# Attention followed by hashed experts on one core: rows of x of four sequences kept on the chip and written later, gathers and weight loads in another order

## The chip, the cores and the metric

The kernel runs on one core of a Trainium2 chip. The metric is the time of one execution on the device in microseconds (us), less is better. Shorthand used throughout: PE is TensorE, PEld its weight loads, DVE VectorE, ACT ScalarE, POOL GpSimd, SP SyncE. Sequences are numbered 0 to 7 and experts 0 to 7.

## What is computed

Two stages, the second fed by the first. Attention over 8 sequences of 576 positions and 8 heads of 64, causal by blocks of 64; then each of the 4608 rows of 512 numbers goes through the one expert that its token id selects:

```python
scores = (q @ k.T) / sqrt(64);  scores = where(block_i >= block_j, scores, -1e9)
x   = softmax(scores) @ v                       # 8 sequences x 576 rows, heads side by side: [4608, 512]
e   = token_ids * 2654435761 % 8                # one expert for each row
out = relu(x @ w1[e]) @ w2[e]                   # w1[e]: 512 x 1024, w2[e]: 1024 x 512
```

## The kernel before, in words

**Attention.** One loop (L597) runs over g = 0 to 33. Pair g (two heads of sequence g // 4) is scored at step g in three chunks (`S_chunk`, L225: matmuls on PE, then one exponential on ACT, L237), and multiplied by V two steps later (`PV`, L263), after which `norm` (L281) divides on DVE and puts the rows into a buffer `xs` on the chip. A sequence fills four steps, so the rows of sequence b are complete at step 4b+5. `T_sixth` transposes q and k of the next sequence on PE.

**Loads and stores around it.** K and Q come by POOL's DMA queue (`load_seq`, L547, at the first step of a sequence), V by SP's queue (`load_v`, L135, six transfers into one of two buffers `vf`, then cast by POOL, `cast_v`, L151). Also on SP's queue, `write_x(b)` (L294, called at L641 in step 4b+5) writes the rows of sequence b to `x_dram` in two transfers. There are two buffers `xs`. An engine's queue is followed in program order: an instruction that waits holds up what stands behind it.

**Experts.** Routing gives each expert five tiles of 128 rows: tiles 0 to 2 hold rows of sequences 0 to 5 only, tiles 3 and 4 the remainder. I write (e,t) for tile t of expert e. `load_x` (L304) gathers a tile from `x_dram` by an indirect DMA of POOL: for tiles 0 to 2 it needs the written rows of sequences 0 to 5, for tiles 3 and 4 all rows. `turn_x` (L501) transposes a gathered tile on PE, DVE copies it into `xT`. `stage_a` (L669) is the first product with the ReLU on ACT, `stage_b` (L693) the second, each of its tiles being scattered to the output by an indirect DMA of POOL (L709). `load_w1` and `load_w2` (L483, L488) bring an expert's weights, 2 MB each in HBM, converted to 1 MB of bf16 on the way, by POOL's queue. I write w1(e) and w2(e) for them.

**The join of the two**, in which most of the change lies. In the loop's last steps, on POOL: w1(0) at step 25, held by L647 until a part of V of sequence 7 has landed; cast of V of sequence 7 at step 26; gathers (0,0), (0,1), (0,2), (1,0), (1,1), (1,2) one each at steps 27 to 32, each held until the last exponential of its step (`last`, L617); w1(1) at step 28; w2(0) at step 32; w2(1) at step 33. On PE: `turn_x` of (0,0) and (0,1) at the end of step 30 and of (0,2) at the end of step 31; three of the eight parts of `stage_a` of expert 0 at step 32. Behind the loop (L741 on): the other five parts of `stage_a(0)` with the turns of (1,0), (1,1), (1,2) between them and, on POOL, the gathers (2,0), (2,1), (2,2); then on POOL (0,3), (0,4), (1,3), (1,4); on PE `stage_a(1)` for three tiles, `stage_b(0)` for three tiles with the turns of (0,3), (0,4); then the loop over the experts (L746), which starts with the last two tiles of expert 0. `xT` and `hT` of experts 0 and 1 lie in a pool of their own (`fst`, two buffers), those of later experts in `mx`, which is opened where the attention's buffers were.

Of the kernel before, what the change touches and what calls it, by code (L numbers as in the profile page):

```python
# [11 lines left out]
BF16 = mybir.dt.bfloat16  # L12
# [5 lines left out]
B, H, S, D = 8, 8, 576, 64  # L18
E, DM, FF = 8, 512, 1024
N = B * S  # L20
NT = 4
NP = H // 2
# [3 lines left out]
G = CAP // 128  # L26
# [12 lines left out]
def kernel(  # L39
# [11 lines left out]
    P = nc.NUM_PARTITIONS  # L51
# [6 lines left out]
    xin = ctx.enter_context(tc.tile_pool(name="xin", bufs=3))  # L58
    fst = ctx.enter_context(tc.tile_pool(name="fst", bufs=2))

# [42 lines left out]
    def after(ins, first, why):  # L103
        tc.add_manual_dep(ins.ins, first.ins.name, SYNC, reason=why)
# [14 lines left out]
    pt4s = [fix.tile([P, NP * 64 + 64], BF16, name=f"pt4{z}") for z in range(2)]  # L119
    xss = [fix.tile([P, 5, DM], BF16, name=f"xs{z}") for z in range(2)]  # L120

# [159 lines left out]
    def norm(g):  # L281
        b, r = divmod(g, NP)
        Ov = Os.pop(g)[:, :, 0 : 5 * (D + 1)].rearrange("p m (t c) -> p m t c", t=5)
        rs = rsall[:, g, :, :]
        nc.vector.reciprocal(rs, Ov[:, :, :, D])  # L285
        nc.vector.tensor_tensor(  # L286
            out=xss[b % 2][:].rearrange("p t (m r d) -> p m t r d", m=2, r=NP)[:, :, :, r, :],
            in0=Ov[:, :, :, 0:D], in1=rs[:, :, :, None].to_broadcast([P, 2, 5, D]), op=ALU.mult)

    x_writes, x_reads, xgs = [], [], {}  # L290
    GE = ES // P


    def write_x(b):  # L294
        xs = xss[b % 2]
        for dst, src in (
            (x_dram[b * S : b * S + 512, :].rearrange("(i p) c -> p i c", p=P), xs[:, 0:NT, :]),
            (x_dram[b * S + 512 : (b + 1) * S, :], xs[0:64, NT, :]),
        ):
            ins = nc.sync.dma_start(dst, src)  # L300
            for r in x_reads:
                tc.declare_no_dep(ins.ins, r.ins, reason="early slots hold rows of earlier sequences")

    def load_x(e, g0, g1, first=None):  # L304
# [188 lines left out]
    NPAIRS = B * NP  # L493
# [3 lines left out]
    def new_ffn(e, pool):  # L497
        xTs[e] = pool.tile([P, NKT, CAP], BF16, name="xT", tag="xT")
        hTs[e] = pool.tile([P, NFT, CAP], BF16, name="hT", tag="hT")
# [15 lines left out]

    for e in range(2):
        new_ffn(e, fst)

# [78 lines left out]
    for g in range(NPAIRS + 2):  # L597
# [30 lines left out]
        if g == NPAIRS - 2:  # L628
            for tt in range(GE - 1):
                turn_x(0, tt, psT)  # L630
        if g == NPAIRS - 1:
            turn_x(0, GE - 1, psT)
        if g == NPAIRS:
# [4 lines left out]
        if r == 0 and b + 2 < B:  # L638
            load_seq(b + 2)
        if r == 1 and g > 1:  # L640
            write_x((g - 5) // NP)  # L641

        c = b + 2 if b + 2 < B - 1 else b + 1 if b + 1 == B - 1 else B
        if r == 1 and c < B:
            vparts[c] = load_v(c)
        if r == 1 and c == B - 1:
            after(load_w1(0), vparts[c][1], "these bytes are wanted first")  # L647
        if r == 2 and b + 1 < B:
            cast_v(b + 1)

        gx = g - (NPAIRS - 5)
        if 0 <= gx < 2 * GE:
            load_x(gx // GE, gx % GE, gx % GE + 1, last)
        if g == NPAIRS - 4:
            load_w1(1)
        if g == NPAIRS:
            load_w2(0)
        if g == NPAIRS + 1:
            load_w2(1)
    assert next(rgen, None) is None and rgen.gi_frame is None  # L660
# [58 lines left out]
    def sums_in_range():  # L719
# [19 lines left out]
        nc.vector.tensor_single_scalar(ctl[:, 3:4], nov[:], float(E * G), op=ALU.add)  # L739

    stage_a(0, 0, ES, EARLY, [(1, tt) for tt in range(GE)], [(2, tt) for tt in range(GE)])  # L741
    for e in range(2):
        load_x(e, GE, G)
    stage_a(1, 0, ES)
# [209 lines left out]
```

## Time and profile before

| what | value |
|---|---|
| median of 3 runs | 304.59 us (302.82 to 308.38) |
| the profiled execution, its own time | 303.5 us |
| the same, span from first to last instruction | 301.7 us |
| granted clock of TensorE, mean over the span | 0.972 |
| PE busy | 263.5 us, 87% of the span |
| ACT busy, DVE busy, POOL busy | 148.7, 141.0, 134.7 us |
| DMA | 55.63 MB, 184 GB/s over the span |

The profiled execution has 1.8 us outside its span (303.5 against 301.7). PE is busy for 87% of the span, with a matmul's end modelled, so what counts is where it is idle and what ended that idle time. A line of a timeline gives the start, the duration, the engine, the line of the kernel, the operation with its output and input, how many instructions are merged into it, and in brackets the idle time before it with what ended it.

### The profile page before, as it was taken

The numbers are of one execution on the slowest core, as the hardware profiler recorded it, in microseconds if no ns is written. First come the engines' busy times: TensorE is split into PE (matmuls) and PEld (weight loads), VectorE is DVE, ScalarE is ACT, GpSimd is POOL, SyncE is SP. The second block draws the span as 40 slices with busy tenths as digits, with TensorE's granted clock in tenths as the row PEclk, the third lists the DMA queues.
The fourth block names the chain that finished last, engine by engine and source line by source line (L and its number), as shares of the span: only waits on it lengthen the run. The fifth ranks groups of instructions, "written<-read, shape, count | busy, mean of one in ns | idle before, by whom it ended". The sixth has DMA issues, their size and how long they took to land. (4 is left out here: it accounts for less than half of the span.)

```text
span 301.7 us, 7635 instructions
## 1 busy us (share of the span) xinstructions
PE 263.5 (87%) x3224; PEld 172.8 (57%) x3241; DVE 141.0 (47%) x296; ACT 148.7 (49%) x192; POOL 134.7 (45%) x164
## 2 busy tenths in 40 slices
PE   7778889899989797459959999999999999999992
PEld 2456667676767575246516656657466575665740
DVE  6787788887889693214012242150421504215131
ACT  3698697888987789234604303306034060240610
POOL 8153250514141304652266735674756738435132
PEclk9999999999999999778979999999999999999997
DMA  6999999999999959979924999699796998942012
GB/s 101 205 184 181 224 174 240 192 233 193 223 214 235 176 149 182 230 146 175 233 70 139 189 226 224 226 185 275 157 202 230 192 269 185 219 187 116 36 72 87
DMA packets 65383, 55.63 MB, mean 184 GB/s; under 512 B 39989, under 2 KB 54325, under 8 KB 65344
## 3 DMA queue, kind: packets, MB, share of 16 engines
q0 software_dynamic: 22832, 40.90, 64.9%
q1 hardware_dynamic: 42512, 14.20, 20.8%
q8 instruction: 26, 0.43, 0.6%
q14 instruction: 13, 0.11, 0.1%
HBM read 67.15 MB, written 15.20 MB: 273 GB/s over the span
## 5 line engine op out<-in xcount | busy, mean ns | idle before, releaser
L237 ACT ACTIVATE pt<-ps 128x1024 bf16<-128x1024 f32 x96 | 92.2, 1026 | 23.2 <-PE ps L220 22.4
L683 ACT ACTIVATE hT<-hp 128x640 bf16<-128x640 f32 (+2 forms) x77 | 46.3, 601 | 102.2 <-PE hp L679 101.4
L700 PE MATMUL yp<-w2b,hT 128*128 128x512 bf16 x305 | 75.7, 385 | 0.8
L679 PE MATMUL hp<-xT,w1b 128*128 128x320 bf16 (+2 forms) x500 | 71.8, 298 | 3.0 <-DVE xT L506 2.8
L506 DVE COPY xT<-tx 128x512 bf16<-128x512 bf16 x40 | 17.0, 424 | 107.0 <-PE tx L504 107.0
L709 POOL DMA_INDIRECT out_dram<-ysb,perm x40 | 39.8, 996 | 50.4 <-DVE ysb L707 22.9
L679 PEld LDWEIGHTS <-w1b 128*128 128x128 bf16 x500 | 48.3, 97 | 23.5 <-issue 6.0
L309 POOL DMA_INDIRECT xg<-x_dram,tabi x40 | 41.1, 1027 | 33.0 <-issue 10.7
L700 PEld LDWEIGHTS <-hT 128*128 128x128 bf16 x320 | 30.4, 99 | 30.7 <-issue 1.5
L211 PE MATMUL ps<-qkT 64*128 64x512 bf16 (+4 forms) x320 | 39.0, 300 | 8.1 <-ACT pt L237 5.1
L186 DVE COPY qkT<-tp 128x768 bf16<-128x768 bf16 x42 | 38.3, 951 | 7.8 <-PE tp L179 7.8
L275 PE MATMUL O<-vx,pt 128*128 128x65 bf16 x896 | 40.2, 197 | 1.9 <-DVE xs L286 1.7
L275 PEld LDWEIGHTS <-pt 128*128 128x128 bf16 x896 | 32.6, 99 | 7.9 <-DVE xs L286 2.6
L211 PEld LDWEIGHTS <-qkT 64*128 64x128 bf16 x320 | 19.2, 94 | 22.2 <-issue 9.5
L111 POOL DMA_DIRECT2D kb<-in_k_dram x9 | 6.7, 748 | 53.8 <-PE O L278 25.0
L707 DVE COPY ysb<-yp 128x512 f32<-128x512 f32 x40 | 27.3, 682 | 6.1 <-PE yp L700 6.1
L286 DVE TENSOR_TENSOR xs<-O,rsall 128x640 bf16<-128x640 f32 x32 | 26.4, 824 | 1.1
L504 PE MATMUL tx<-identbf,xg 128*128 128x128 bf16 x160 | 15.9, 225 | 11.3 <-DMA xg<-x_dram,tabi 11.3
L504 PEld LDWEIGHTS <-xg 128*128 128x128 bf16 x160 | 12.5, 101 | 20.6 <-DMA xg<-x_dram,tabi 12.1
L220 PE MATMUL ps<-maskq,maskk 64*128 64x64 bf16 x256 | 23.1, 191 | 0.0
L154 POOL CAST vx<-vf 128x2048 bf16<-128x2048 f32 x8 | 15.3, 1916 | 7.3 <-DMA vf<-in_v_dram 2.8
L285 DVE RECIPROCAL rsall<-O 128x10 f32<-128x10 f32 x32 | 7.0, 219 | 18.8 <-PE O L278 18.0
(142 smaller groups left out, 179.9 us busy)
## 6 DMA issues: line engine op xcount, KB each, us to landing
vf<-in_v_dram SPq DMA_DIRECT2D x32, 256.0 KB, 9.3
w1b<-in_moe_w_dram POOLq DMA_DIRECT2D x8, 1024.0 KB, 8.4
w2b<-in_moe_w_dram POOLq DMA_DIRECT2D x8, 1024.0 KB, 13.6
x_dram<-xs SPq DMA_DIRECT2D x8, 512.0 KB, 9.9
kb<-in_k_dram POOLq DMA_DIRECT2D x7, 576.0 KB, 7.2
qb<-in_q_dram POOLq DMA_DIRECT2D x6, 576.0 KB, 10.1
vf<-in_v_dram SPq DMA_DIRECT2D x16, 64.0 KB, 4.4
qb<-in_q_dram POOLq DMA_DIRECT2D x2, 320.0 KB, 8.1
```

Of the source, the lines that this page charges most:

```text
L186: ins = copy(qk[:, :, w, :].rearrange("p h (g j) -> p h g j", j=JR)[:, :, :, j0 + c0 : j0 + c1], tp[:, at[c0] : at[c1 - 1] + 1, :].rearran ...
L211: nc.tensor.matmul(ps[:, m, o0 : o0 + n], lhsT=qk[rows, r, 1, 128 * i : 128 * i + 128], rhs=qk[rows, r, 0, q0 : q0 + n], start=True, stop= ...
L237: return nc.scalar.activation(ptv[:, :, 512 * ch : 512 * ch + 512], ps[:], ACT.Exp, scale=SCALE)
L275: nc.tensor.matmul(dst, lhsT=pt[:, o0 : o0 + 128], rhs=vx[:, h, i, :], start=(i == 0), stop=(i == t))
L286: nc.vector.tensor_tensor(out=xss[b % 2][:].rearrange("p t (m r d) -> p m t r d", m=2, r=NP)[:, :, :, r, :], in0=Ov[:, :, :, 0:D], in1=rs[ ...
L309: r = nc.gpsimd.indirect_dma_start(out=xgs[e][:, gg, :], out_offset=None, in_=x_dram[0:rows, :], in_offset=bass.IndirectOffsetOnAxis(ap=ta ...
L504: nc.tensor.transpose(out=tp[:, db, :], in_=xgs[e][:, tt, db * P : (db + 1) * P], identity=identbf[:])
L679: nc.tensor.matmul(hp[:, t, 0:n], lhsT=w1b[:, db, ft * P : (ft + 1) * P], rhs=xT[:, db, p0:p1], start=(db == 0), stop=(db == NKT - 1),)
L683: relu = nc.scalar.activation(hT[:, ft, c0:c1].rearrange("p (t n) -> p t n", n=n), hp[:, 0 : len(parts), 0:n], ACT.Relu)
L700: nc.tensor.matmul(yp[:], lhsT=hT[:, ft, tt * P : (tt + 1) * P], rhs=w2b[:, ft, :], start=(ft == 0), stop=(ft == NFT - 1),)
L707: nc.vector.tensor_copy(ysb[:], yp[:])
L709: ins = nc.gpsimd.indirect_dma_start(out=out[:, :], out_offset=bass.IndirectOffsetOnAxis(ap=perm3[:, gg : gg + 1], axis=0), in_=ysb[:], in ...
```

## The change

Eight edits. (1) Five buffers `xs` in place of two; the rows of sequences 2 to 5 stay in them and are all written at step 25, in place of steps 13, 17, 21 and 25. Those of sequences 0, 1, 6 and 7 are written at the steps they had. (2) V of sequence 7 is asked for at step 21 in place of step 25. (3) `fst` has one buffer; `xT` and `hT` of expert 1 come from `mx`. (4) Gathers one step later: (0,0) at step 28 to (1,0) at step 31, with (1,1) and (1,2) both at step 32. (5) w1(0) moves from step 25 to step 28, behind gather (0,0), and loses its hold on V; w1(1) moves from step 28 to step 30, behind gather (0,2). (6) On PE, (0,0) alone is turned at step 30; (0,1) and (0,2) at step 31. (7) w2(1) moves from step 33 to behind the gathers (0,3), (0,4), and waits until the rows of sequence 7 are written; (1,3), (1,4) come behind it. (8) w2(0) keeps step 32, now behind two gathers there.

```diff
--- before.py
+++ after.py
@@ -56,7 +56,7 @@
     dram = ctx.enter_context(tc.tile_pool(name="dram", bufs=1, space=DRAM))
     wts = ctx.enter_context(tc.tile_pool(name="wts", bufs=3))
     xin = ctx.enter_context(tc.tile_pool(name="xin", bufs=3))
-    fst = ctx.enter_context(tc.tile_pool(name="fst", bufs=2))
+    fst = ctx.enter_context(tc.tile_pool(name="fst", bufs=1))
 
     x_dram = dram.tile([N, DM], BF16, name="x_dram")
     a_dram = dram.tile([B * H, S, D], BF16, name="a_dram")
@@ -117,7 +117,8 @@
         vexts.append((vx, v4))
     pts = [fix.tile([P, 2 * PTW + 64], BF16, name=f"pt{z}") for z in range(3)]
     pt4s = [fix.tile([P, NP * 64 + 64], BF16, name=f"pt4{z}") for z in range(2)]
-    xss = [fix.tile([P, 5, DM], BF16, name=f"xs{z}") for z in range(2)]
+    XB = 5
+    xss = [fix.tile([P, 5, DM], BF16, name=f"xs{z}") for z in range(XB)]
 
     def set_fixed():
         for vx, v4 in vexts:
@@ -284,7 +285,7 @@
         rs = rsall[:, g, :, :]
         nc.vector.reciprocal(rs, Ov[:, :, :, D])
         nc.vector.tensor_tensor(
-            out=xss[b % 2][:].rearrange("p t (m r d) -> p m t r d", m=2, r=NP)[:, :, :, r, :],
+            out=xss[b % XB][:].rearrange("p t (m r d) -> p m t r d", m=2, r=NP)[:, :, :, r, :],
             in0=Ov[:, :, :, 0:D], in1=rs[:, :, :, None].to_broadcast([P, 2, 5, D]), op=ALU.mult)
 
     x_writes, x_reads, xgs = [], [], {}
@@ -292,7 +293,7 @@
 
 
     def write_x(b):
-        xs = xss[b % 2]
+        xs = xss[b % XB]
         for dst, src in (
             (x_dram[b * S : b * S + 512, :].rearrange("(i p) c -> p i c", p=P), xs[:, 0:NT, :]),
             (x_dram[b * S + 512 : (b + 1) * S, :], xs[0:64, NT, :]),
@@ -300,6 +301,7 @@
             ins = nc.sync.dma_start(dst, src)
             for r in x_reads:
                 tc.declare_no_dep(ins.ins, r.ins, reason="early slots hold rows of earlier sequences")
+        return ins
 
     def load_x(e, g0, g1, first=None):
         if e not in xgs:
@@ -513,8 +515,7 @@
                 start=(db == 0), stop=(db == NKT - 1))
         nc.scalar.activation(hTs[e][:, ft, 0:ES], hp[:, 0:ES], ACT.Relu)
 
-    for e in range(2):
-        new_ffn(e, fst)
+    new_ffn(0, fst)
 
     J2 = 8
     EARLY = 3
@@ -626,10 +627,10 @@
         turn(0)
 
         if g == NPAIRS - 2:
-            for tt in range(GE - 1):
+            turn_x(0, 0, psT)
+        if g == NPAIRS - 1:
+            for tt in range(1, GE):
                 turn_x(0, tt, psT)
-        if g == NPAIRS - 1:
-            turn_x(0, GE - 1, psT)
         if g == NPAIRS:
             for ft in range(EARLY):
                 stage_a_early(0, ft)
@@ -637,26 +638,22 @@
             next(rgen, None)
         if r == 0 and b + 2 < B:
             load_seq(b + 2)
-        if r == 1 and g > 1:
-            write_x((g - 5) // NP)
-
-        c = b + 2 if b + 2 < B - 1 else b + 1 if b + 1 == B - 1 else B
-        if r == 1 and c < B:
-            vparts[c] = load_v(c)
-        if r == 1 and c == B - 1:
-            after(load_w1(0), vparts[c][1], "these bytes are wanted first")
+        if r == 1 and b + 2 < B:
+            vparts[b + 2] = load_v(b + 2)
+
+        if r == 1:
+            for c in {5: (0,), 9: (1,), 25: (2, 3, 4, 5), 29: (6,), 33: (7,)}.get(g, ()):
+                rows = write_x(c)
         if r == 2 and b + 1 < B:
             cast_v(b + 1)
 
-        gx = g - (NPAIRS - 5)
-        if 0 <= gx < 2 * GE:
-            load_x(gx // GE, gx % GE, gx % GE + 1, last)
-        if g == NPAIRS - 4:
-            load_w1(1)
+
+        for e, tt in {28: ((0, 0),), 29: ((0, 1),), 30: ((0, 2),), 31: ((1, 0),), 32: ((1, 1), (1, 2))}.get(g, ()):
+            load_x(e, tt, tt + 1, last)
+        if g in (28, 30):
+            load_w1((g - 28) // 2)
         if g == NPAIRS:
             load_w2(0)
-        if g == NPAIRS + 1:
-            load_w2(1)
     assert next(rgen, None) is None and rgen.gi_frame is None
     att_ctx.close()
 
@@ -738,9 +735,11 @@
         nc.vector.tensor_scalar(ctl[:, 2:3], nb[:, 0:1], float(-E * G), float(E * G), op0=ALU.mult, op1=ALU.add)
         nc.vector.tensor_single_scalar(ctl[:, 3:4], nov[:], float(E * G), op=ALU.add)
 
+    new_ffn(1, mx)
     stage_a(0, 0, ES, EARLY, [(1, tt) for tt in range(GE)], [(2, tt) for tt in range(GE)])
-    for e in range(2):
-        load_x(e, GE, G)
+    load_x(0, GE, G)
+    after(load_w2(1), rows, "the rows are wanted first")
+    load_x(1, GE, G)
     stage_a(1, 0, ES)
     stage_b(0, 0, GE, [(0, tt) for tt in range(GE, G)])
     for e in range(E):
```

## Rows read from the trace of the kernel before

**Rows 1.** Busy time by stretch: window, five engines (instructions), granted clock, DMA share, GB/s.

```profile
105.00:110.00 5.00, 4.51 (x104) 3.41 (x102) 4.83 (x8) 3.96 (x5) 0.00 (x0) 1.00 0.36 116
...
125.00:130.00 5.00, 3.69 (x43) 2.49 (x44) 0.85 (x2) 1.94 (x2) 1.39 (x2) 0.50 0.99 162
...
155.00:160.00 5.00, 5.00 (x22) 2.21 (x21) 2.14 (x4) 0.00 (x0) 2.75 (x3) 0.66 0.43 131
```

**Rows 2.** Timeline of PE, join of the two stages and the third expert.

```profile
126.31 1.04 PE L504 MATMUL tx<-identbf,xg 128*128 128x128 bf16 x8 [4.48 <-DMA xg<-x_dram,tabi]
...
134.05 0.40 PE L504 MATMUL tx<-identbf,xg 128*128 128x128 bf16 x4 [3.10 <-DMA xg<-x_dram,tabi]
...
135.58 3.39 PE L511 MATMUL hp<-xT,w1b 128*128 128x384 bf16 x12
...
142.37 7.02 PE L679 MATMUL hp<-xT,w1b 128*128 128x384 bf16 x40
...
154.85 0.40 PE L504 MATMUL tx<-identbf,xg 128*128 128x128 bf16 x4 [3.73 <-DMA xg<-x_dram,tabi]
155.08 3.46 PE L700 MATMUL yp<-w2b,hT 128*128 128x512 bf16 x8
...
160.44 4.24 PE L679 MATMUL hp<-xT,w1b 128*128 128x256 bf16 x32
...
193.89 0.39 PE L504 MATMUL tx<-identbf,xg 128*128 128x128 bf16 x4
```

**Rows 3.** Timeline of POOL: DMA issues of weights, gathers, scatters.

```profile
115.02 0.78 POOL L486 DMA_DIRECT2D w1b<-in_moe_w_dram  x1 [13.95 <-DMA vf<-in_v_dram]
...
123.20 0.83 POOL L486 DMA_DIRECT2D w1b<-in_moe_w_dram  x1
...
152.07 1.01 POOL L309 DMA_INDIRECT xg<-x_dram,tabi  x1 [6.91 <-DMA x_dram<-xs]
...
162.57 0.86 POOL L486 DMA_DIRECT2D w1b<-in_moe_w_dram  x1
...
190.54 0.99 POOL L709 DMA_INDIRECT out_dram<-ysb,perm  x1 [4.04 <-DMA w2b<-in_moe_w_dram]
```

**Rows 4.** DMA issues of single transfers, KB each, us from issue to landing.

```profile
w1b<-in_moe_w_dram POOLq DMA_DIRECT2D x1, 1024.0 KB, 8.5
...
w1b<-in_moe_w_dram POOLq DMA_DIRECT2D x1, 1024.0 KB, 10.4
...
w2b<-in_moe_w_dram POOLq DMA_DIRECT2D x1, 1024.0 KB, 9.0
xg<-x_dram,tabi POOLq DMA_INDIRECT x1, 2.8
...
kb<-in_k_dram POOLq DMA_DIRECT2D x1, 576.0 KB, 8.0
```

**Rows 5.** Timeline of SP's queue.

```profile
95.39 13.10 SPq L300 DMA_DIRECT2D x_dram<-xs  x4
...
120.12 21.88 SPq L300 DMA_DIRECT2D x_dram<-xs  x4
```

**Rows 6.** Timeline of ACT: last exponentials of steps 28, 29 and 30.

```profile
116.03 0.41 ACT L250 ACTIVATE pt<-ps 128x256 bf16<-128x256 f32 x1
116.73 5.65 ACT L237 ACTIVATE pt<-ps 128x1024 bf16<-128x1024 f32 x6 [0.29 <-PE ps L220]
```

**Rows 7.** DMA queues over 111-116, 125-131.5 and 143-151 us: packets, MB, share of engines.

```profile
q1 hardware_dynamic: 4067, 1.04, 91.6%
...
q0 software_dynamic: 551, 1.16, 99.9%
...
q0 software_dynamic: 982, 1.23, 78.1%
q1 hardware_dynamic: 608, 0.59, 25.3%
```

**Rows 8.** Timeline of PE: first use of K of sequence 7.

```profile
103.63 0.86 PE L179 MATMUL tp<-identbf,kb 128*64 128x128 bf16 x24 [1.04 <-DMA kb<-in_k_dram]
```

## The prediction, as it was made

> **What bounds the kernel now.** I read the stretches first [rows 1], then PE's timeline where the clock or the DMA share falls, then the queues that feed it. Three things are to be seen.
>
> PE is the bound nearly everywhere, but at the join of the two stages it waits three times for a gather: 4.48 us before 126.31, 3.10 before 134.05, 3.73 before 154.85, 11.3 us in all [rows 2]. After these waits it runs at the lower of its two clocks for a while: granted 0.50 in 125 to 130 and 0.66 over 155 to 160 [rows 1]. The price: twelve matmuls of 384 columns took 3.39 us where forty at full clock took 7.02, so 2.1 for twelve: 1.3 lost; eight of 512 columns took 3.46, by the same rate (512/384 of 0.176 us each) 1.9: 1.6 lost [rows 2]. With about 1.3 after the first wait, the three cost about 4 us more. So of PE's 38.6 us from 121.83 (126.31 less its wait) to 160.44 some 15.5 are no work.
>
> Why the gathers are late is in POOL's queue [rows 3]. w1(0) waited 13.95 us for V of sequence 7, and the cast and gather (0,0) stand behind it. V was itself late: on SP it stands behind the write of sequence 5, which waits for the last row of that sequence (the four transfers of two writes take 13.10 us, to 108.5 [rows 5]), while the DMA engines are 0.36 busy [rows 1]. The second wait is one of order: w1(1), issued at 123.20, landed 10.4 later, at 133.6, and gather (0,2), issued right behind it, was there at 134.05 [rows 2 to 4]: a gather lands behind the weights queued ahead of it. The third: the writes of sequence 7 were issued by 142.0 [rows 5] and POOL saw them landed at 152.07 [rows 3]; w2(0) and w2(1) shared the engines with them.
>
> **The parts, in the order of time** (times on the axis of before).
>
> Writes kept back. A written row packet costs 0.253 x 8 us x 16 / 608 = 0.053 us of one engine [rows 7], so the 576 packets of a sequence 1.9 us of all 16, four sequences 7.7. In steps 13 to 21 they leave the loads alone; I price that at nothing, since K came only 1.0 us late for sequence 7 [rows 8] and the exponentials pace those steps. Bounds: a gain of that 1.0 us, a loss in the rival on K below.
>
> V of sequence 7. It now waits on SP for no row, only for its buffer and V of sequence 6 ahead of it. 4067 packets of V took 91.6% of 5 us [rows 7], so all 4608 take 5.2. SP was through with V of sequence 6 by 95.4 [rows 5]; without writes ahead, I take V of 7 as landed by 100 to 104. POOL's 13.95 us wait goes. Next on SP: sequences 2, 3, 4 go at once, sequence 5 when its last row is there (108.5, as before); at 1.9 us each all four have landed by about 113. Gather (0,0) is asked for only after that.
>
> Gather (0,0). POOL is free; it waits for the last exponential of step 28, done at 116.0 [rows 6]. Alone a gather takes 2.8 [rows 4]: there at 119, and PE turns it at 121.83 without a wait. The 4.48 us go.
>
> w1(0). Issued behind it at 117.1, in place of 115.02. It took 8.5 [rows 4]: 125.6, and the write of sequence 6, issued from 120.12 [rows 5], adds up to 1 us: 126.6. Gathers (0,1), (0,2), issued at 119.6 and 122.4 after the exponentials of steps 29 and 30 (thirds of the 5.65 us [rows 6]), stand behind it: there at 127 to 129, I take 128.0. PE, with one turn at 121.83 and step 31 behind it (2.8 us, half of the 5.65 for two steps' exponentials [rows 6]), is at that turn by 124.6. New wait: 3.4. It is of the length that lowered the clock before, so I add 1.6.
>
> Then on PE: of its 23.1 us of work up to 160.44 (38.6 less 15.5), sixteen parts of stage_a and three tiles of stage_b take 16.8 by the rate above and step 31 2.8, which leaves 3.5 for eight turns and the last two steps' PVs. I take 2.2 of these here, with three parts of stage_a 4.3, and the slow 1.6: 133.9; one part more: 134.5. w1(1) starts on the engines when w1(0) and the two gathers are through, about 126.6; 551 packets took 99.9% of 6.5 us, so its 512 take 6.0 [rows 7], with some 2 to land, and 0.5 for the gather: (1,0) at about 135.4. New wait 0.9. The cover of w1(1) itself is that it is wanted only by stage_a(1).
>
> w2(0). It starts behind (1,2) and, by the 9.0 of before [rows 4] less some 1.5 us from issue to first packet, lands 7.5 after 135, plus 1.9 for the rows of sequence 7: 144.4 to 145. PE has five parts of stage_a(0), three turns and the eight parts of stage_a(1) before it: 144.0. New wait about 0.6. The rows of sequence 7 are issued at 135, not 141, and share with one w2, not two: landed by 143.8 (8.8 us, before 10). (0,3) then lands at 146.7, when PE has its first tile of stage_b(0) done: about 0.2. The 3.73 us go, with their slow clock.
>
> w2(1) behind the rows. Issued at 146.5, wanted by stage_b(1) at 163. That is covered, but (1,3), (1,4) and everything later on POOL's queue stand behind its 6.5 us (982 packets of such traffic took 78.1% of 8 us [rows 7], so 1024 take 6.5): (1,3) at 156.3, where PE wants it at 156.5. Before, w1(2) went out at 162.57 onto idle engines, and w2(3) had landed 28 us later, at 190.54 [rows 3]; gather (3,0), right behind, was turned at 193.89 [rows 2], some 3 us of slack. After, w1(2) reaches the engines when w2(1), two gathers and three scatters are through, as if issued at about 155: w2(3) at 183, 7.5 earlier. PE may be up to 10.5 earlier there before it waits. I take 0.5 for waits at (2,3) and (3,0); bounds 0 and 4.
>
> Covered at nothing: xT(1), hT(1) in mx need the last readers of K, Q and the V buffers, all done by 120, 15 us before their first write; without that cover the copy of (1,0) would wait and PE with it. The eight transfers on SP at step 25 delay nothing there: the next write on SP comes at 120.12 [rows 5].
>
> **The sum**, against the profiled execution's 303.5 (span 301.7 and 1.8 around it). Gone: 11.3 + about 4 = 15.5. New: 3.4 + 1.6 + 0.9 + 0.6 + 0.2 = 6.7, later 0.5. Net 15.5 - 7.2 = 8.3: 295.2. The median of the runs shown lies 1.1 above the profiled execution, within their spread; I predict 295.2 for the median.
>
> **A rule weighed.** The third and fourth of rows 7, taken together, show 982 packets of POOL's queue and 608 of SP's served in the same 8 us, 1.6 to 1: neither is served first to the end. The Trainium skill (DMA: Bandwidth & Descriptors, Queues, rings and completion order) says that each engine goes round-robin between the queues that have work, packet by packet. By that rule K and Q of sequence 7 lose one row packet to each of theirs when the held writes meet them, under 1 us; the trace agrees as far as it goes. The same skill (Trainium Kernel Development and Optimization, Key Constraints) says that transfers issued from several queues run on the same 16 engines and interleave, so the writes are only moved; that speaks for the second rival below.
>
> **The rivals.**
> (a) The gathers do not queue behind w1(0) and land 2.8 after issue [rows 4]: (0,2) at 125.5, a wait of 0.9 in place of 3.4 and no slow clock. 295.2 - 2.5 - 1.6 = 291. Against it: 133.6 and 134.05 above. Chance 0.15.
> (b) The bytes are only moved and the engines become the bound: the new wait for w2(1), which before had landed in the shadow, sets every later load back. With w2(1) through 3 to 4 us later than I take, PE waits at (1,3), (2,3), (3,0) for as much: 299. For it: from w1(2) to w2(3) the engines stood still for almost nothing, and POOL itself waited for w2 at 190.54 [rows 3]. Chance 0.22.
> (c) Slower. V of sequence 7 and three writes are served before K of sequence 7, which landed 8.0 after its issue [rows 4] and was 1.0 late already [rows 8]: 5.2 + 3 x 1.9 = 10.9 us of stall at 103.63, so 306. It decides from a delay of 8.3 on. Against it: rows 7, third and fourth. Chance 0.06.
>
> **How the numbers follow.** Forecast 0.57 (its own range 292.5 to 298.5), (a) 0.15, (b) 0.22, (c) 0.06. The range of 290.5 to 300.5 takes in (a) and most of (b) and leaves out (c) and the tails. Some 2% is what a measurement here can tell from no change: 298.5. Nearly all of the forecast, (a) and a sixth of (b) lie below: faster 0.74; the remainder of (b), the forecast's tail and a mild (c) within 2%: 0.20; slower 0.06.
>
> **What would show it.** Right: no wait of POOL for V; PE's turn at step 30 without idle time; one wait of 3 to 4 us at the turn of (0,1), (0,2), ended by the gather, with one stretch of lower clock; stage_a of expert 0's last tiles starting some 9 us before 160.44. Wrong: a wait for K near 103 of over 3 us; idle PE at turns of experts 2 and 3 of over 2 us; (0,1) there by 124; a wait at the first copy into xT(1).

## The result: 294.9 us, and the profile after

The changed kernel takes 294.93 us (median; 294.21 to 295.09) where the kernel before took 305.75 over all its runs beside it (302.82 to 308.38): a ratio of 0.967, 95% interval 0.959 to 0.976. Executions fall into a faster and a slower state, and ratios here and below are of the faster ones alone, so a ratio can differ from that of the two medians beside it. The profiled execution took 294.84 us with a span of 293.2, against 303.5 and 301.7. That is 8.7 us less between the two profiles and 10.8 between the medians; the profiled execution of before lay 2.2 under this median, and in two later comparisons the changed kernel's medians were 8.2 under those of before (298.92 against 307.07, 298.79 against 307.00). So 8 to 9 us is the size to explain. PE is busy for 260.7 us, 89% of the span.

The stretches of [rows 1], in the changed kernel, with two more between them (window, the five engines' busy time, granted clock, DMA share, GB/s):

```profile
105.00:110.00 5.00, 3.77 (x82) 2.76 (x78) 4.88 (x8) 3.54 (x5) 2.63 (x3) 1.00 0.95 307
...
115.00:120.00 5.00, 4.03 (x83) 3.03 (x83) 2.09 (x4) 4.71 (x6) 2.35 (x3) 1.00 0.21 34
125.00:130.00 5.00, 1.21 (x15) 1.12 (x16) 1.00 (x3) 0.08 (x1) 4.03 (x4) 0.82 1.06 272
130.00:135.00 5.00, 5.00 (x74) 3.78 (x71) 1.65 (x5) 1.47 (x3) 0.00 (x0) 0.83 1.11 247
...
155.00:160.00 5.00, 4.29 (x26) 2.07 (x25) 1.27 (x3) 0.64 (x2) 3.03 (x4) 1.00 1.09 310
```

The DMA engines, 0.36 busy in 105 to 110 before, are now full there with the end of V and the rows, and are free (0.21) when gather (0,0) goes out. From 125 on they are full again: that is the stretch in which PE now waits.

PE's timeline of the changed kernel, the lines that answer to [rows 2] (start, duration, engine and line, operation, idle time before it and what ended it):

```profile
121.38 0.39 PE L506 MATMUL tx<-identbf,xg 128*128 128x128 bf16 x4
...
128.79 1.05 PE L506 MATMUL tx<-identbf,xg 128*128 128x128 bf16 x8 [4.46 <-DMA xg<-x_dram,tabi]
...
131.30 2.38 PE L513 MATMUL hp<-xT,w1b 128*128 128x384 bf16 x12
...
135.43 0.40 PE L506 MATMUL tx<-identbf,xg 128*128 128x128 bf16 x4 [0.15 <-DMA xg<-x_dram,tabi]
...
147.12 0.40 PE L506 MATMUL tx<-identbf,xg 128*128 128x128 bf16 x4 [0.92 <-DMA xg<-x_dram,tabi]
...
151.03 4.24 PE L676 MATMUL hp<-xT,w1b 128*128 128x256 bf16 x32
...
157.37 0.40 PE L506 MATMUL tx<-identbf,xg 128*128 128x128 bf16 x4 [0.37 <-DMA xg<-x_dram,tabi]
```

The turn of (0,0) waits for nothing. The turn of (0,1) and (0,2) waits 4.46 us; those of (1,0), (0,3) and (1,3) wait 0.15, 0.92 and 0.37. Expert 0's last two tiles start at 151.03, where before it was 160.44 [rows 2]: 9.4 earlier.

POOL's timeline of the same kernel, the lines that answer to [rows 3]:

```profile
106.93 1.90 POOL L155 CAST vx<-vf 128x2048 bf16<-128x2048 f32 x1 [9.85 <-DMA vf<-in_v_dram]
...
116.75 1.10 POOL L311 DMA_INDIRECT xg<-x_dram,tabi  x1 [7.13 <-DVE rsall L286]
117.86 0.82 POOL L488 DMA_DIRECT2D w1b<-in_moe_w_dram  x1
...
123.40 0.81 POOL L488 DMA_DIRECT2D w1b<-in_moe_w_dram  x1
...
144.22 1.01 POOL L311 DMA_INDIRECT xg<-x_dram,tabi  x1 [4.41 <-DMA x_dram<-xs]
...
146.54 0.96 POOL L493 DMA_DIRECT2D w2b<-in_moe_w_dram  x1
```

And the landings of what was issued in 117 to 121, the one w1 among them being w1(0) and the write that of sequence 6 (KB each, us from issue to landing; the 6.0 of the two gathers is the middle between 2.9 for (0,0) and 9.2 for (0,1)):

```profile
w1b<-in_moe_w_dram POOLq DMA_DIRECT2D x1, 1024.0 KB, 10.4
x_dram<-xs SPq DMA_DIRECT2D x1, 512.0 KB, 12.2
x_dram<-xs SPq DMA_DIRECT2D x1, 64.0 KB, 12.8
xg<-x_dram,tabi POOLq DMA_INDIRECT x2, 6.0
```

Gather (0,1) by itself, issued at 119.57 behind w1(0):

```profile
xg<-x_dram,tabi POOLq DMA_INDIRECT x1, 9.2
```

So w1(0) landed at 128.3 and (0,1) at 128.8, just behind it.

The account between the two profiles: idle time at the turns 4.46 + 0.15 + 0.92 + 0.37 = 5.9 us against 11.3 [rows 2], 5.4 less; matmuls at the lower clock cost about 1.1 us (0.83 over 130 to 135, so 0.17 x 5.00, and 1.05 for eight transposes where two fours at full clock take 0.79) against about 4, 2.9 less; attention 0.3 less (step 28, the first of sequence 7, starts at 115.00, before at 115.30). Together 8.6 of 8.66. Whether each of these parts is worth on its own what it says here is what the experiments ask.

### The profile page after: what moved, and what is told of

It reads as the page before. It is cut to its first block, busy times and chain, and to the rows that moved or that the text cites. A ratio compares the mean times of both kernels' runs of the same rounds, so it can differ in the third digit from the quotient of the medians.

```text
span 293.2 us, 7638 instructions
## 1 busy us (share of the span) xinstructions
PE 260.7 (89%) x3224; PEld 171.9 (59%) x3241; DVE 140.8 (48%) x296; ACT 148.6 (51%) x192; POOL 133.8 (46%) x164
## 5 line engine op out<-in xcount | busy, mean ns | idle before, releaser
L697 PE MATMUL yp<-w2b,hT 128*128 128x512 bf16 x305 | 74.2, 379 | 0.8
L706 POOL DMA_INDIRECT out_dram<-ysb,perm x40 | 39.8, 995 | 47.0 <-DMA xg<-x_dram,tabi 19.9
L212 PE MATMUL ps<-qkT 64*128 64x512 bf16 (+4 forms) x320 | 38.9, 298 | 8.2 <-ACT pt L238 5.1
## 6 DMA issues: line engine op xcount, KB each, us to landing
vf<-in_v_dram SPq DMA_DIRECT2D x32, 256.0 KB, 10.3
```

The source lines that it names most:

```text
L212: nc.tensor.matmul(ps[:, m, o0 : o0 + n], lhsT=qk[rows, r, 1, 128 * i : 128 * i + 128], rhs=qk[rows, r, 0, q0 : q0 + n], start=True, stop= ...
L697: nc.tensor.matmul(yp[:], lhsT=hT[:, ft, tt * P : (tt + 1) * P], rhs=w2b[:, ft, :], start=(ft == 0), stop=(ft == NFT - 1),)
L706: ins = nc.gpsimd.indirect_dma_start(out=out[:, :], out_offset=bass.IndirectOffsetOnAxis(ap=perm3[:, gg : gg + 1], axis=0), in_=ysb[:], in ...
```

## The experiments

Two accounts stand against each other. By the first, the late V of sequence 7 is what makes the first gather late, and V early, with the rows kept to make room for it, brings most of the gain. By the second, the engines from the first gather on work through a line of transfers, and it is their order that counts, whatever PE or a single early load does.

In what follows the *join* is the time from the start of step 28 on PE (its 64x64 matmuls, at 115.00 in the changed kernel) to the end of the profiled execution; in this way a delay within attention drops out. It is 188.2 us before and 179.8 after. Medians are compared with runs of the kernel before on the same chip: 305.46 for the first four kernels, 307.07 for the next four, 307.00 for the last four.

**1. V of sequence 7 early, nothing else.** The kernel before, with V of 7 asked for at step 21 behind the write of sequence 4; w1(0) stays at step 25 and stays held by V.

```diff
-        c = b + 2 if b + 2 < B - 1 else b + 1 if b + 1 == B - 1 else B
-        if r == 1 and c < B:
-            vparts[c] = load_v(c)
-        if r == 1 and c == B - 1:
+        if r == 1 and b + 2 < B:
+            vparts[b + 2] = load_v(b + 2)
+        if g == 25:
             after(load_w1(0), vparts[7][1], "these bytes are wanted first")
```

> The kernel before with one edit: V of sequence 7 is asked for at step 21 in place of step 25 (its own two xs buffers, its writes and its order of gathers and weights stay). My theory: V's place behind the write of sequence 5 on SP's queue is what held POOL for 13.95 us, not the bytes of the writes. So POOL issues w1(0) by about 107, gathers (0,0) and (0,1) are there before 121.8, the wait of 4.48 us and its stretch of lower clock go; (0,2) still stands behind w1(1), which is now early too, and is there at about 126 (wait some 2 us). The wait for (0,3) stays at 3 to 5 us, since w2(0) and w2(1) still share the engines with the rows of sequence 7. Profiled execution 295 to 297. Rival (the rows kept on the chip are what frees the engines): V and K of sequence 7 come late behind the writes, POOL still waits over 5 us for V, 300 or more.

Measured: 306.04, ratio 1.009 (1.004 to 1.014), no gain; the join 187.0. POOL's timeline of this kernel, and behind it the line of gather (0,0) in the kernel before:

```profile
111.99 0.78 POOL L486 DMA_DIRECT2D w1b<-in_moe_w_dram  x1 [8.87 <-DMA vf<-in_v_dram]
114.65 1.89 POOL L154 CAST vx<-vf 128x2048 bf16<-128x2048 f32 x1 [1.89 <-PE ps L220]
...
121.22 0.41 POOL L157 CAST v<-vf 64x256 bf16<-64x256 f32 x1 [4.33 <-DMA vf<-in_v_dram]
124.71 1.10 POOL L309 DMA_INDIRECT xg<-x_dram,tabi  x1 [3.08 <-ACT pt L237]
```

```profile
120.74 1.10 POOL L309 DMA_INDIRECT xg<-x_dram,tabi  x1 [0.63 <-ACT pt L237]
```

w1(0) went out 3.0 us sooner than before, and the last part of V, 64 KB asked for 0.6 us ahead of it, landed 9.7 after its issue and kept POOL waiting 4.33 more; the write of sequence 5 beside it took 10.5 (before 5.0). Gather (0,0) was issued 4.0 us later than before, or 2.0 later when counted from the start of step 28. PE waited 3.82, 1.04, 2.46 and 3.05 for gathers. That V is asked for late is thus not the cause by itself: what stands ahead of the first gather gets in the way. V asked for early was not there early, though: its cast was done at 121.6, before at 120.1. What V there early is worth, this run does not show; the next one does.

**2. Rows kept and V early, the old order.** The changed kernel with edits 4 to 8 undone.

```diff
-        for e, tt in {28: ((0, 0),), 29: ((0, 1),), ...}.get(g, ()):
-            load_x(e, tt, tt + 1, last)
-        if g in (28, 30):
-            load_w1((g - 28) // 2)
+        gx = g - (NPAIRS - 5)
+        if 0 <= gx < 2 * GE:
+            load_x(gx // GE, gx % GE, gx % GE + 1, last)
+        if g == NPAIRS - 4:
+            load_w1(1)
...
+        if g == 25:
+            after(load_w1(0), vparts[7][1], "these bytes are wanted first")
```

> The changed kernel with the old order of gathers, turns and weight loads (edits 4 to 8 undone): rows of sequences 2 to 5 kept and written at step 25, V of sequence 7 early, xT and hT of expert 1 in mx. My theory: as e1 within 1 us, because only V's place counts; first wait gone, (0,2) at about 126, (0,3) late by 4 us with a stretch of lower clock: 294.5 to 297. Rival (the new order carries the gain): only the first wait of 4.5 us and 1.3 of lower clock go, 298 to 299. Rival (kept rows free the engines): clearly below e1, by 2 us or more.

Measured: 303.54, ratio 1.000 (0.996 to 1.005); the join 187.4. On POOL:

```profile
104.76 0.78 POOL L488 DMA_DIRECT2D w1b<-in_moe_w_dram  x1 [6.93 <-DMA vf<-in_v_dram]
107.26 1.89 POOL L155 CAST vx<-vf 128x2048 bf16<-128x2048 f32 x1 [1.73 <-DMA vf<-in_v_dram]
...
122.48 1.10 POOL L311 DMA_INDIRECT xg<-x_dram,tabi  x1 [9.91 <-DVE rsall L286]
```

and the landings of what was issued in 104 to 108, the kept rows among it:

```profile
w1b<-in_moe_w_dram POOLq DMA_DIRECT2D x1, 1024.0 KB, 10.9
x_dram<-xs SPq DMA_DIRECT2D x2, 512.0 KB, 11.0
vf<-in_v_dram SPq DMA_DIRECT2D x2, 64.0 KB, 5.9
x_dram<-xs SPq DMA_DIRECT2D x2, 64.0 KB, 10.4
```

w1(0) is asked for 10.3 us sooner than before and V is cast by 112.6, yet gather (0,0) goes out at 122.48, 1.7 later than before. In the changed kernel the transfers of the same kept rows land 3.3 to 5.9 us after issue, here 7.1 to 11.2. By the sizes of the prediction, w1(0) with 6.0 us of all engines and four sequences of rows with 7.7 fill them from 105 to 119, and with some 2 us to land the rows are there at 121. The brackets name DVE as what released the gather. The rows fit better: the last of them landed at 121.3, 1.2 us ahead of the gather, and the same 1.2 lie between that landing and the gather in experiments 6, 11 and 12, where the brackets name ACT, DVE and nothing. PE waited 3.29, 0.71, 2.61 and 3.81: the waits of before in other places. So keeping rows and V early, which I had thought of as the first half of the gain, are worth nothing under the old order.

**3. The new order alone.** The changed kernel with edits 1 to 3 undone: two buffers, the old writes, V of 7 behind the write of sequence 5.

```diff
-        if r == 1 and b + 2 < B:
-            vparts[b + 2] = load_v(b + 2)
...
+        c = b + 2 if b + 2 < B - 1 else b + 1 if b + 1 == B - 1 else B
+        if r == 1 and c < B:
+            vparts[c] = load_v(c)
```

> The kernel before with only the new order of gathers, turns and weight loads (edits 4 to 8 without mx): two xs buffers, old writes, V of sequence 7 at step 25. My theory: gather (0,0) waits for V's cast until 120.7 and is there at 123.6, a wait of 1.8 us at its turn; (0,1) and (0,2) behind w1(0) at about 131, wait 4 to 5 us; the wait for (0,3) shrinks to about 1. About 297.5, so a large part of the gain without the kept rows. Rival (V's place is all that counts): 301 to 304, since POOL is still held by V.

Measured: 301.98 (297.87 to 305.00), ratio 0.990 (0.984 to 0.996). The profiled execution, 303.28, lies above the median, so only its order is read:

```profile
122.17 1.90 POOL L155 CAST vx<-vf 128x2048 bf16<-128x2048 f32 x1 [18.90 <-DMA vf<-in_v_dram]
```

on POOL, and on PE

```profile
129.82 0.61 PE L506 MATMUL tx<-identbf,xg 128*128 128x128 bf16 x4 [2.36 <-DMA xg<-x_dram,tabi]
...
137.18 1.03 PE L506 MATMUL tx<-identbf,xg 128*128 128x128 bf16 x8 [3.50 <-DMA xg<-x_dram,tabi]
```

With V late the cast still stands in POOL's queue ahead of gather (0,0) and PE waits for it (2.36); w1(0), behind the gather, is then late too. The new order is worth about 1% by itself, some third of the whole.

**4. The new order and V early, the writes at their old steps.** Sequences 2 to 5 are written at steps 13 to 25, each ahead of the V asked for in that step.

```diff
+        if r == 1:
+            for c in {5: (0,), 9: (1,), 13: (2,), 17: (3,), 21: (4,), 25: (5,), 29: (6,), 33: (7,)}.get(g, ()):
+                rows = write_x(c)
         if r == 1 and b + 2 < B:
             vparts[b + 2] = load_v(b + 2)
```

> The changed kernel with every write of rows at its old step (13, 17, 21 and 25 for sequences 2 to 5, and ahead of V in its step); five buffers, early V and the new order stay. My theory: the place of the writes is worth nothing to 1 us: 294 to 296, POOL's first gather at the same 116.8, K of sequence 7 late by under 2 us. Rival (keeping the rows back is what frees the engines for the loads): V of sequence 7 lands after 110, K of sequence 7 is late by 3 us or more, 298 or more.

Measured: 298.19, ratio 0.984 (0.977 to 0.991); the join 179.2, as in the changed kernel, with one wait left at the turns, 4.26 at that of (0,1) and (0,2). What it lost lies elsewhere: step 28 starts at 119.41, and the largest wait on the way is

```profile
35.35 1.49 PE L180 MATMUL tp<-identbf,kb 128*64 128x128 bf16 x24 [2.28 <-DMA kb<-in_k_dram]
```

That is some 30 us ahead of step 13, the first step at which its writes differ from those of the changed kernel. Of the two orders at SP only the turn of V and write within a step differs by then. So this left two readings: the place of the writes costs 3 us in attention, or loads at the start of a run vary. The first write of this kernel went out at 40.5, behind that wait, which speaks for the second. Experiments 9 and 10 go back to it.

**5. The changed kernel again**, beside the next three.

> The changed kernel once more, unchanged, beside the other runs on the same chip. e1 and e2 made my first theory fall: V's early place alone gained nothing, since the engines served K, Q and the writes of sequences 3 and 4 with it, and the kept rows alone gained nothing, since w1(0), issued at 104.8, ran ahead of them. New theory: the gain needs the kept writes and w1(0) behind gather (0,0) together, because w1(0) and the rows of sequences 2 to 5 compete for the engines in 105 to 115. Expected here: 294 to 297, a ratio to before of 0.96 to 0.975. Rival (the earlier result was that chip's): as e4, 297.5 to 299.

Measured: 298.92 (297.15 to 300.44), ratio 0.976 (0.968 to 0.985); profiled 297.15, join 180.9, waits 4.38, 0.39, 0.21. That median is 4.0 above the one of the first comparison, that of before only 1.3, so the size of the gain itself varies, from 8.2 to 10.8 us between medians.

**6. w1(0) one step earlier**, at step 27, ahead of gather (0,0) and without the hold on V.

```diff
-        if g in (28, 30):
-            load_w1((g - 28) // 2)
+        if g in (27, 30):
+            load_w1((g - 27) // 3)
```

> The changed kernel with w1(0) issued at step 27, in front of gather (0,0), in place of step 28. One theory (the 4.46 us wait for (0,1), (0,2) is there because they queue behind w1(0)): w1(0) goes out at about 110 and is in by 119; the rows of sequence 5 land some 4 us later, at 118 to 119, (0,0) at 121.5 to 122.5 with a wait of up to 1.1 at step 30; (0,1), (0,2) have nothing ahead of them and are there by 125.4, wait at most 1.2; no stretch of lower clock: 290 to 292. Rival (rows that share the engines with w1(0) come late, as in e2): the rows land at 120 or later, (0,0) after 123, and what is gained at step 31 is lost at step 30: 294 to 298.

Measured: 300.62, ratio 0.979 (0.971 to 0.987); the join 185.5, 4.6 more than in the changed kernel beside it. POOL's timeline:

```profile
110.81 0.78 POOL L488 DMA_DIRECT2D w1b<-in_moe_w_dram  x1
122.79 1.10 POOL L311 DMA_INDIRECT xg<-x_dram,tabi  x1 [11.21 <-ACT pt L238]
```

and PE's:

```profile
126.10 0.61 PE L506 MATMUL tx<-identbf,xg 128*128 128x128 bf16 x4 [3.29 <-DMA xg<-x_dram,tabi]
...
130.12 1.04 PE L506 MATMUL tx<-identbf,xg 128*128 128x128 bf16 x8
```

Two things. A wait of 3.29 stands at (0,0): with rows still to be written when w1(0) started, the last of them landed 10.1 after issue and the gather went out 6 us later than in the changed kernel. This is experiment 2 in small: ahead of the first gather, the load also delays the rows that the gather needs. And the wait of 4.4 at the turn of (0,1) and (0,2) is gone. That alone does not show that w1(0) had been in their way, since PE, held at (0,0), came to this turn 13.8 us after the start of step 28, as in the changed kernel; the landing of (0,1) right behind w1(0) there does. The 4.6 us are between single profiles; the medians lie 1.7 apart, and the two intervals overlap.

**7. w2(1) back at step 33**, ahead of the rows of sequence 7.

```diff
         if g == NPAIRS:
             load_w2(0)
+        if g == NPAIRS + 1:
+            load_w2(1)
...
-    after(load_w2(1), rows, "the rows are wanted first")
```

> The changed kernel with edit 7 undone: w2(1) issued at step 33, right behind w2(0), without waiting for the rows of sequence 7. My theory: the rows of sequence 7 share the engines with w2(1) and land 2 to 3 us later than 144.2, gather (0,3) comes at about 149.5 in place of 147.1; PE waits 3 to 3.5 us for it in place of 0.92 and runs a stretch at the lower clock; the 0.37 us for (1,3) go: 297.5 to 299.5, 3 to 4 above e5. Rival (edit 7 is worth nothing): within 1 us of e5.

Measured: 300.60 (300.38 to 300.84), ratio 0.981 (0.973 to 0.988); the join 185.3, 4.4 more than beside it, though the median is only 1.7 more. POOL's timeline, then PE's:

```profile
146.51 1.01 POOL L311 DMA_INDIRECT xg<-x_dram,tabi  x1 [5.96 <-DMA x_dram<-xs]
```

```profile
149.95 0.40 PE L506 MATMUL tx<-identbf,xg 128*128 128x128 bf16 x4 [2.98 <-DMA xg<-x_dram,tabi]
```

The rows of 7 land 8.6 after issue, not 7.5; (0,3) goes out at 146.51, 2.3 later, and PE waits 2.98 for it, where it had waited 0.92. So edit 7 takes away the third wait of [rows 2], as the prediction had it.

**8. The wait filled.** Fourteen matmuls, whose results nothing reads, in front of the turn of (0,1), so that PE is not idle and its clock stays up.

```diff
         if g == NPAIRS - 1:
+            fill(14)
             for tt in range(1, GE):
                 turn_x(0, tt, psT)
```

> The changed kernel with 14 idle matmuls of 512 columns (about 3.1 us, results unread) on PE at the end of step 31, in front of the turn of (0,1), inside the wait of 4.46 us; nothing else moves. My theory: PE's idle time before the turn falls to about 1.4 us, the clock stays granted at 1.0 through 125 to 135 (0.82 and 0.83 without them), and the first matmuls behind the turn take their full-clock times: 1.0 to 1.5 us less than e5. Rival (the lower clock costs nothing on the path, since the next wait takes it up): within 0.5 us of e5.

Measured: 298.20, ratio 0.973 (0.965 to 0.981), 0.7 below the kernel beside it, with executions that overlap. The granted clock is 1.00 in 125 to 130 and in 130 to 135, where the kernel beside it (experiment 5) had 0.70 and 0.61, and 0.993 over the span. PE:

```profile
129.38 0.84 PE L506 MATMUL tx<-identbf,xg 128*128 128x128 bf16 x8 [1.33 <-DMA xg<-x_dram,tabi]
...
136.09 0.40 PE L506 MATMUL tx<-identbf,xg 128*128 128x128 bf16 x4 [1.28 <-DMA xg<-x_dram,tabi]
...
148.07 0.40 PE L506 MATMUL tx<-identbf,xg 128*128 128x128 bf16 x4 [1.21 <-DMA xg<-x_dram,tabi]
```

PE began the last PVs 17.8 us after the start of step 28, against 19.0 in the changed kernel, so the write of sequence 7 was issued 1.2 sooner. It landed hardly sooner (0.2): 8.5 us after issue instead of 7.5, and (0,3) went out at 29.5 after the start of step 28, against 29.2. What the clock gave, the next waits took: 1.28 for (1,0) and 1.21 for (0,3). The row write runs beside w2(0), and the two are through at about the same time (in the changed kernel w2(0) at 129.0 + 13.0 = 142, the write at 135.8 + 7.5 = 143.3).

**9 and 10. Experiment 4 again beside the changed kernel.**

> The kernel of e4 (the changed kernel with every write of rows at its old step) beside the changed kernel on one chip. e4's profile lost 3.8 us in attention, at a late K, and nothing at the join. One theory (the kept rows free the engines during attention, where they were full, so that K comes in time on every chip and run): here again 1.5 to 4 us above e10 in the median, with waits of PE for K or Q between 25 and 110 us, and a join as in e10 within 1 us. Rival (e4's late K was chance, the place of the writes is worth nothing): median within 1 us of e10.

> The changed kernel, unchanged, as the reference of this call: 294 to 299, 0.965 to 0.98 of the kernel before. Theory: waits of PE at the join 4.4 us for (0,1), (0,2), under 1 us each elsewhere. Rival: none; the run sets the level for the three beside it.

Measured: 299.47 (297.06 to 300.84), ratio 0.974 (0.969 to 0.978), for the old writes; 298.79 (295.75 to 300.43), ratio 0.971 (0.966 to 0.976), for the changed kernel. The joins are 181.1 and 181.4. With the old writes step 28 again starts later, 119.04 against 116.27. The delay is there by the start of sequence 1 (33.8 against 30.5), ahead of the first write, at 41.2. Between the medians lie 0.7 us, well inside either spread: what keeping the rows is worth, once the order is new and V early, is not shown.

**11 and 12. Gather (0,0) and w1(0) one step earlier, and the write of sequence 6 later.** At step 27 the gather waits only for its rows, not for the exponential of step 28; in 12 the write of sequence 6, which is issued 2 us behind w1(0), moves to step 31.

```diff
+        if g == 27:
+            load_x(0, 0, 1)
-        if g in (28, 30):
-            load_w1((g - 28) // 2)
+        if g in (27, 30):
+            load_w1((g - 27) // 3)
```

and in 12 besides

```diff
-            for c in {5: (0,), 9: (1,), 25: (2, 3, 4, 5), 29: (6,), 33: (7,)}.get(g, ()):
+            for c in {5: (0,), 9: (1,), 25: (2, 3, 4, 5), 33: (7,)}.get(g, ()):
                 rows = write_x(c)
+        if g == 31:
+            write_x(6)
```

> The changed kernel with gather (0,0) and w1(0) at step 27, the gather held by nothing but the written rows (in the changed kernel it waits for the last exponential of step 28, done 1 to 2 us after the rows had landed, while the engines stood at 0.21). Theory (the join goes at the pace of POOL's transfers from gather (0,0) on; e8 gained nothing on PE's side): w1(0) goes out about 2 us earlier, still behind the rows, and (0,1), (0,2), w1(1), (1,0), w2(0) with it; the wait at step 31 falls from 4.4 to 2 to 3 us; 1 to 2.5 us under e10. Rival (what is gained is lost again, as in e6, since w1(0) now meets other traffic): within 1 us of e10 or above it.

> e11 and the write of sequence 6 at step 31 in place of 29, so that it no longer shares the engines with w1(0) (its rows are wanted only by gather (0,3)). Theory: w1(0) and the gathers behind it land 1 to 1.9 us earlier than in e11, the wait at step 31 falls by as much; the rows of sequence 6 then share with w1(1), whose gather (1,0) had 0.15 us of wait, so half of it comes back there: 0.5 to 1.5 us under e11. Rival (the same bytes in the same stretch): within 0.5 us of e11.

Measured: 296.85 (295.47 to 298.70), ratio 0.967 (0.963 to 0.970), and 296.76 (295.44 to 299.64), ratio 0.968 (0.963 to 0.973). The joins are 181.4 and 180.3. Gather (0,0) went out 1.2 and 1.0 us after the start of step 28, against 1.75 in experiment 10; in 11:

```profile
117.07 1.10 POOL L311 DMA_INDIRECT xg<-x_dram,tabi  x1 [6.57 <-DVE rsall L286]
```

so it gained 0.6 to 0.7 us of some 2 expected. The trace names DVE, but it is the rows that hold it: their last transfer landed at 115.90 (64 KB issued at 111.21, 4.7 to landing), 1.17 us ahead of the gather, and 1.17 lie between the two in 12 as well (117.02 and 118.19), where the trace names no releaser. In experiment 10 the rows had landed 1.42 ahead of the gather, so there were only some 0.25 us to gain from the exponential. The edit of 12 did not move the write: it was issued 4.8 us after the start of step 28 in 11 and in 12, as soon as its rows were complete, since nothing stands ahead of it on SP. What w1(0) would take without that write is thus not tested. The wait for (0,1) is 3.77 and 3.58 in place of 4.31. The medians are 1.9 and 2.0 below that of experiment 10, with runs that overlap: too little to call either better than the changed kernel.

## What sets the join

One table of profiled executions shows it (us after the start of step 28):

| kernel | (0,3) turned at | join |
|---|---|---|
| before | 39.6 | 188.2 |
| 1: V early, nothing else | 39.8 | 187.0 |
| 2: rows kept, V early, old order | 38.9 | 187.4 |
| 7: changed, w2(1) early | 34.8 | 185.3 |
| 6: changed, w1(0) ahead of the gather | 34.7 | 185.5 |
| changed kernel, three profiles | 32.1, 32.0, 32.1 | 179.8, 180.9, 181.4 |
| 8: changed, wait filled | 32.4 | 182.0 |
| 4 and 9: changed, old writes | 32.1, 32.3 | 179.2, 181.1 |
| 11 and 12: changed, (0,0) earlier | 31.9, 31.4 | 181.4, 180.3 |

The turn of (0,3) moves with the order of the transfers and not with PE: a faster PE (8) or another place for the row writes (4, 9) leaves it within 0.4 us, a weight load set ahead of rows or gathers (6, 7) costs 2.6 to 2.8 there and 4 to 5 by the end of these profiled executions (1.7 between the medians). So I read the join from gather (0,0) on as a line of transfers, which rests on experiment 8 for PE's part: rows of 0 to 5, (0,0), w1(0), (0,1), (0,2), w1(1), and w2(0) beside the rows of 7. Neither half of the change gives more than 1% alone (1 to 3); V early and the order together (4, 9) give 1.6 and 2.6, where the whole change gave 2.4 to 3.3.

## Why the prediction was right, and where not

The time: 295.2 predicted, 294.9 measured; gone and new sum to 8.3 predicted, 8.7 between the profiles. That the median came within 0.3 us is in part luck: between medians the gain was 10.8 here and 8.2 in the two later comparisons, and errors of single terms cancel, as the list shows. The mechanism holds in its main steps, with two terms mis-sized and one misplaced.

- *K of sequence 7, rival (c).* The wait of 1.04 [rows 8] is gone, and none came. The rival fell.
- *V of 7 landed by 100 to 104.* Its cast waited until 106.93: 3 us late, since V shared the engines with K and Q until 101 (last section), and at no cost, since POOL next waited 7.13 for the gather. But the step that ties the first wait to V's place was half a cause. Experiments 1 and 2 ask for V early and leave the turn of (0,0) within 1.0 us of where it was (10.4 and 10.0 us after the start of step 28, before 11.0), because w1(0), freed with it, then shares with V's last part or the rows. The prediction let that load move behind the gather in the same breath and so never priced one without the other.
- *(0,0) issued 116.0, turned at 121.83 without a wait.* Issued 116.75, turned 121.38, no wait: right.
- *(0,1), (0,2) there at 128.0, wait 3.4.* There at 128.8, wait 4.46: right in kind, so rival (a) fell: (0,1) landed right behind w1(0), 9.2 after its issue. The term that failed is w1(0)'s: 8.5 plus up to 1, measured 10.4, and it was issued at 117.86, not 117.1. The prediction put the "up to 1" down to the write of sequence 6. That this write is what lengthened w1(0) is not shown: by 125.0 only 15 of its 576 packets had begun (last section), and experiment 12, meant to take it away, left it where it was. The cause stays open.
- *The slow clock, 1.6.* About 1.1 in the matmuls (some 2.0 in experiment 5, by 0.61 over 130 to 135), but experiment 8, in which it is gone, is not faster by more than 0.7 us, with executions that overlap. So far as these runs can tell the term was no part of the path: the next transfer was waited for. By the same token the 2.9 us of slow clock in the account above are not an independent gain; they went with the waits.
- *(1,0) 0.9, w2(0) 0.6, (0,3) 0.2, later 0.5.* Measured 0.15, none, 0.92, and 0.37 at (1,3); 1.4 for 2.2. With the 4.46 and the 1.1 the new costs sum to 7.0 where 7.2 was predicted: the single terms miss by up to 1.1, in both directions. Edit 7 was rightly named as what removes the third wait (experiment 7).
- *Rival (b), the engines the bound later on.* There is no wait at (2,3) or (3,0): the stage_a lines of before at 169.10, 183.61 and 202.59 come at 160.23, 174.74 and 193.72, all 8.9 earlier. Right that the slack was enough. In the join, though, (b) had a point: there the transfers do set the pace.
- *Writes kept back, priced at nothing.* From the first sequence's 64x64 matmuls to step 28 attention takes 100.2 us before and 100.1 after, so the price of nothing holds; by experiments 9 and 10 it is worth no more than can be measured. The writes of sequences 0 and 1 were kept back too, though their steps stay: behind V on SP they went out at 51.9 and 66.0, before at 39.4 and 53.4. That edit is the first half of the title, and the others carry the gain.

What stays open: what the 1.17 us between the rows' landing and gather (0,0) are, and what lengthened w1(0); why attention took 2 to 4 us longer in three profiles (3, 4, 9), in the latter two lost before a first write went out; and whether kept rows are worth anything under 1 us.

## What to carry to other kernels

Where several queues feed one set of DMA engines, write down what is wanted next and by when, and let no bulk load start ahead of the small transfers that stand before the next piece of work, nor ahead of the writes that those need. Test such a change whole and in parts: here the parts alone were worth at most 1%, the whole 2.4 to 3.3%. And before crediting a faster engine or a restored clock, ask which transfer it will then wait for.

## What the runs showed of the hardware

In two stretches two queues took turns packet by packet, whatever the size of the packets. In the changed kernel, in 95 to 101 us, POOL's queue (q0) had K and Q of sequence 7 and SP's (q1) V of it (packets, MB, share of engines):

```profile
q0 software_dynamic: 481, 1.07, 93.0%
q1 hardware_dynamic: 508, 0.13, 15.9%
```

The counts are nearly equal, so V, with packets of 256 B, moved 0.13 MB where K and Q moved 1.07. In experiment 2, in 111 to 113, w1(0) and the rows had 113 packets each. The Trainium skill (DMA: Bandwidth & Descriptors, Queues, rings and completion order) says that an engine changes between the queues it has work for after each packet. The trace agrees in these two stretches; the prediction used this rule only for the rows against K, where it cost nothing, and not for V against K and Q.

A write issued behind a weight load began late. The write of sequence 6 landed 12.2 us after issue with w1(0) beside it and 5.7 before; w1(0) took 10.4 instead of 8.5. The write was issued at 119.83, and this ran in 120 to 125:

```profile
q0 software_dynamic: 386, 0.79, 103.6%
q1 hardware_dynamic: 15, 0.02, 1.1%
```

Most of its 576 packets ran in 125 to 130, 573 on SP's queue against 367, and the last ones beside w1(1). So the 12.2 us are not the price of taking turns with all of w1(0). Why the first packets came so late, and what w1(0) lost its 1.9 us to, these runs do not show.

The lower clock after a wait of 4.4 us cost about 1.1 us in matmuls (2.0 in experiment 5) and no time that these runs can tell: with it gone (granted clock 0.993), the kernel took 298.20 against 298.92, intervals 0.965 to 0.981 and 0.968 to 0.985 of the kernel before.
